# A three-block kernel in float32r parts: low parts of the normalised values on VectorE instead of GpSimd, and the output weights' conversion behind the input projection

## The chip, the cores and the metric

The kernel runs on one core of a Trainium2 chip. The metric is device time in microseconds (us). The engines are TensorE (PE; PEld are its weight loads), VectorE (DVE), ScalarE (ACT), GpSimd (POOL) and SyncE (SP), which issues most of the DMAs. Each engine works through its own instructions in the order in which they stand, and waits for the others by semaphores.

## The reference

Two sequences of 768 tokens with 8 heads of 48 go through three blocks: a linear attention with a state that decays, a Fourier mixing with an MLP, and a spatially gated MLP. The change lies in the third:

```python
def _moe2_ref(x, w_in, g_ln, w_sg, b_sg, w_out):
    h = x @ w_in                                   # [2, 768, 384] @ [384, 1024]
    h = gelu_tanh(h)
    u, v = (h[..., :d_ff // 2], h[..., d_ff // 2:])
    mu = np.mean(v, axis=-1, keepdims=True)
    var = np.mean((v - mu) ** 2, axis=-1, keepdims=True)
    v_n = (v - mu) / np.sqrt(var + 1e-06) * g_ln
    v_s = np.einsum('ts,bsd->btd', w_sg, v_n) + b_sg[None, :, None]
    gated = u * v_s
    return (x + gated @ w_out).astype(np.float32)
```

## The kernel before

TensorE multiplies float32r. To keep float32's precision, every operand of a large product is split in two parts: the high part is the value rounded to float32r, the low part is what is left. A product then takes three matmuls, hi x hi, hi x lo and lo x hi (`mm3`, line 110, where all of them are counted). Names that end in `_hi` and `_lo` are these parts.

The third block is written in `gating`, for batch 0 and then for batch 1:

- `gate_in` makes v for each of six chunks of 128 tokens, t = 0 to 5. TensorE writes `v_ps` (nine matmuls of 512 columns), ScalarE takes the gelu (L575), VectorE the statistics (L577, L579), GpSimd the reciprocal deviation `rs` in two short operations (L581, L582), VectorE normalises in place (L583), ScalarE casts the high part `vn_hi` (L585), and L586 subtracts it to get the low part `vn_lo`.
- `u_in` makes u: eight tiles `u_ps`, nine matmuls of 384 columns each, and a gelu on ScalarE (L596).
- `spatial` multiplies by `w_sg` over the tokens: for each of four feature blocks f and two halves of the tokens, 18 matmuls into `s_ps`, which need vn of all six chunks; then g, b and u on VectorE (L609, L610), and the split of the gated product (L612 on ScalarE, L613 on GpSimd), which takes vn's place.
- `project` multiplies by `w_out` into `o_ps`; VectorE adds x (L624), and a DMA writes the result.

The weights arrive as float64 bits. `load_split` turns 384 columns of them into float32 by three integer operations on VectorE (L157, L158, L159, out `st`), a cast on ScalarE (L163) and a subtraction on GpSimd (L164); `wout` takes four such steps, `late_weights`. `wsg` arrives as float32 and takes a cast and the subtraction only. `raw` and `st` have two buffers each.

Buffers that matter here: the tiles v, t_g and o share the tag "tb" with three buffers, so v of chunk t + 3 may be written when the low part of chunk t has been made. `v_ps`, `u_ps` and `o_ps` share five PSUM banks (tag "g"), `s_ps` has three (tag "c").

The order of instructions isn't that of the code alone. `merge(a, b, 1.0)` writes one step of b behind each step of a, and a list scheduler (Tile, with its own timeline as a guess) then puts the instructions of each engine in order, the earlier written one first where several are ready.

Of the kernel before, what the change touches and what calls it, by code (L numbers as in the profile page):

```python
# [70 lines left out]
# keeps the logarithm finite where a product vanishes  # L71
TINY = 1e-37
# brings any variance into the range of the logarithm
FAR = 2.0 ** -64
# how far a pair's sum over its tokens of P * (1 / P) may lie from their number
# [6 lines left out]
class Split:  # L82
    """An operand as the exact sum of two float32r parts."""
# [13 lines left out]
def fused(ctx, tc, ins, out, dbg=None):  # L97
    nc = tc.nc
# [19 lines left out]
    # ---- constants that stay  # L118
# [27 lines left out]
    def load_split(w, src, o, at, raw=None):  # L146
        """Load NST columns and split them; float64 arrives as raw bits and becomes float32 first."""
# [23 lines left out]
    # ---- attention  # L171
    def prep(n, b, p, ap):
        if b == 0:
            # every pair of the first batch has room of its own: that of later tiles
# [10 lines left out]
        # the first pair in two parts: the start is shorter  # L185
# [10 lines left out]
        for c0, c1 in parts:  # L196
# [6 lines left out]
            # decays from the start of each chunk: P[t] up to before t, P[t + 1] up to and with t  # L203
# [8 lines left out]
            # r and k change sign, both  # L212
# [13 lines left out]
    def own_term(ap, n, b, p, prod, v):  # L226
        """The current token's own term: dv = (sum_d r u k) v."""
# [10 lines left out]
        for c in range(NC_):  # L238
            # the columns after the first two are overwritten: a stream of fewer than 96 takes as long
            nc.tensor.matmul(dg_ps[:, 2 * c:2 * c + 2 * D], lhsT=prod[:, c], rhs=uh[:, None, 2 * p:2 * p + 2].to_broadcast([PR, D, 2]), start=True, stop=True)  # L240
# [8 lines left out]
    def scores(ap, c0, rt, kt):  # L249
        """Scores of chunks c0..c0+2, of the earlier tokens alone."""  # L250
        res = []
        sc_pss = [gps.tile([C, 3, C], F32, name="sc_ps", tag="g") for h in range(2)]
        for i, h in [(i, h) for i in range(3) for h in range(2)] if IL else [(i, h) for h in range(2) for i in range(3)]:
            c = c0 + i
            # the two heads lie in different halves of the array's rows
# [9 lines left out]
    def chunk_states(ap, b, ends, kt, v, U):  # L265
        """States before chunks 1..5: U[j] = P_end[j] * (U[j - 1] + sum_s k v)."""
# [19 lines left out]
    def values(b, c0, rt, sc, v, dv, U, yo):  # L286
        y_ps = ps(b, [C, 512], "y_ps", YB)
        # between the two heads' columns a block that no one reads: both heads' values go through, in the time of one's
# [9 lines left out]
    def radix6(x, y, Z, es, G):  # L298
        """Over the token chunks: x = (a, b), a = y_c + y_c+3, b = +-(y_c - y_c+3);
        Z = sum (Z0, Z3), real (Z2, Z1), imaginary (Z2, Z1; the factors are in the DFT's constants)."""  # L300
# [10 lines left out]
    def attention(ap, yz):  # L311
        """Both batches' pairs of heads, in one pipeline; yields the batch that is through."""
        pairs = [(b, p) for b in range(B) for p in range(NP)]

        def junk(m, l, r):
            """Matmuls that no one reads, where the tensor engine would wait: its clock halves if it idles."""
# [696 lines left out]
```

## Time and profile before

| | |
|---|---|
| median of 3 timed runs | 476.03 us (474.46 to 479.01) |
| span of the profiled execution | 483.4 us; no time of its own is listed beside it |
| TensorE busy | 443.2 us (92%) |
| VectorE busy | 310.9 us (64%) |
| GpSimd busy | 213.1 us (44%) |
| ScalarE busy | 170.0 us (35%) |
| mean granted TensorE clock | 0.881 of full speed |

The profiled execution is another one than the timed ones, and its span is 7.4 us longer than their median. Matmuls are pipelined: a matmul's duration in the timeline is longer than the distance from its start to that of the next, and the distance is what the stream costs. The granted clock is 1.00 (2.4 GHz) or 0.50 (1.2 GHz); a value between is a mean over a stretch. In the timeline the bracket at the end of a row is the time for which the engine stood idle before it, and who released it.

### The profile page before, as it was taken

Reading aid. Unit: us, or ns where it says so; the run is one execution under the profiler, and the core shown is the slowest. Engines: PE = TensorE matmul, PEld = TensorE weight load, DVE = VectorE, ACT = ScalarE, POOL = GpSimd, SP = SyncE. Lnnn points to the kernel's source line nnn. Section 1 sums busy time; section 2 is a strip of 40 time slices with the busy share of each in tenths; the row PEclk is TensorE's granted clock in tenths of the full one; section 3 lists DMA queues with packets and bytes.
Section 4 is the critical chain, followed back from the end, with each engine's and each line's share of the span. In section 5 each row is a group of like instructions: output and inputs, shape, how many; then the busy total and the mean of one; then the engine's idle time right before and its main releaser. Section 6 shows DMA issues by size and latency. Waiting matters only on the chain.

```text
span 483.4 us, 6594 instructions
## 1 busy us (share of the span) xinstructions
PE 443.2 (92%) x2474; PEld 418.3 (87%) x2474; DVE 310.9 (64%) x518; ACT 170.0 (35%) x389; POOL 213.1 (44%) x206
## 2 busy tenths in 40 slices
PE   9689989978869997698999999999999799999995
PEld 8578978977769987598999899999889698999995
DVE  5999799599797899959874531631369334611332
ACT  3542433553543423543424311522364212311110
POOL 1658876468593474634231200201478525700330
PEclk9765555595979999899999999999999799999998
DMA  7932694032225332310050000001333000020002
GB/s 204 273 93 84 204 295 139 1 110 77 68 82 169 127 98 62 77 58 1 6 143 18 0 1 0 1 1 34 95 104 97 0 1 0 18 83 0 2 12 94
DMA packets 13641, 35.41 MB, mean 73 GB/s; under 512 B 1760, under 2 KB 5632, under 8 KB 13472
## 3 DMA queue, kind: packets, MB, share of 16 engines
q1 hardware_dynamic: 13456, 32.54, 22.9%
q0 software_dynamic: 144, 2.36, 1.4%
q8 instruction: 21, 0.34, 0.3%
q14 instruction: 20, 0.16, 0.1%
HBM read 32.53 MB, written 2.36 MB: 72 GB/s over the span
## 4 chain that ended last, share of the span: by engine, by line
PE 48%; DVE 24%; issue 10%; DMA 7%; POOL 6%; ACT 3%; SPq 1%; POOLq 0%; DVEq 0%; ACTq 0%
PE s_ps L110 10%; PE z_ps L110 6%; PE o_ps L110 5%; PE ch L110 5%; PE y_ps L295 4%; PE sc_ps L257 3%; DVE st L158 3%; PE u_ps L110 3%; PE v_ps L110 3%; PE x_ps L110 3%; DMA raw<-in_wsg 2%; DVE st L159 2%; DVE st L157 2%; PE y_ps L293 2%; DMA rk<-in_rk 2%
## 5 line engine op out<-in xcount | busy, mean ns | idle before, releaser
L110 PE MATMUL z_ps<-us_hi,w 128*128 128x384 f32 x288 | 80.7, 344 | 4.2 <-ACT us_hi L499 4.0
L110 PE MATMUL ch<-z_hi,w 128*128 128x384 f32 x288 | 80.5, 339 | 3.1 <-ACT z_hi L523 3.0
L524 DVE SCALAR_TENSOR_TENSOR z_lo<-z_ps,z_hi 128x384 fp32r<-128x384 f32 x48 | 26.6, 554 | 56.1 <-ACT z_hi L523 56.1
L110 PEld LDWEIGHTS z_ps<-us_hi,w 128*128 128x128 f32 x288 | 53.9, 193 | 5.4 <-ACT us_hi L499 4.6
L110 PEld LDWEIGHTS ch<-z_hi,w 128*128 128x128 f32 x288 | 52.4, 189 | 4.8 <-ACT z_hi L523 4.6
L110 PE MATMUL ch<-z_lo,w 128*128 128x384 f32 x144 | 49.2, 342 | 4.1 <-DVE z_lo L524 4.0
L110 PE MATMUL z_ps<-us_lo,w 128*128 128x384 f32 x144 | 48.9, 340 | 0.0
L164 POOL TENSOR_TENSOR w<-st,w 128x384 fp32r<-128x384 f32 x24 | 31.4, 1310 | 31.8 <-ACT w L163 31.8
L523 ACT ACTIVATE z_hi<-z_ps 128x384 fp32r<-128x384 f32 x48 | 23.6, 492 | 59.2 <-PE z_ps L110 45.3
L613 POOL TENSOR_TENSOR vn_lo<-t_g,vn_hi 128x384 fp32r<-128x384 f32 x16 | 16.1, 1016 | 55.6 <-ACT vn_hi L612 55.6
L609 DVE SCALAR_TENSOR_TENSOR t_g<-s_ps,g,bsg 128x384 f32<-128x384 f32 x16 | 9.6, 617 | 47.3 <-PE s_ps L110 47.3
L110 PE MATMUL s_ps<-wsg_hi,vn_hi 128*128 128x384 f32 x96 | 33.7, 351 | 2.7 <-ACT vn_hi L585 2.7
L261 POOL TENSOR_SCALAR_AFFINE_SELECT sc<-sc 128x384 f32<-128x384 f32 x32 | 28.5, 911 | 16.8 <-ACT sc L260 16.6
L110 PE MATMUL s_ps<-wsg_hi,vn_lo 128*128 128x384 f32 x96 | 33.8, 352 | 1.1 <-POOL vn_lo L586 1.1
L110 PE MATMUL s_ps<-wsg_lo,vn_hi 128*128 128x384 f32 x96 | 33.6, 350 | 0.0
L110 PEld LDWEIGHTS ch<-z_lo,w 128*128 128x128 f32 x144 | 27.0, 188 | 6.4 <-DVE z_lo L524 6.3
L295 PE MATMUL y_ps<-v,sc 128*128 128x96 f32 x144 | 28.9, 334 | 0.0
L110 PEld LDWEIGHTS z_ps<-us_lo,w 128*128 128x128 f32 x144 | 27.8, 193 | 0.0
L295 PEld LDWEIGHTS y_ps<-v,sc 128*128 128x128 f32 x144 | 27.2, 254 | 0.6 <-issue 0.4
L164 POOL TENSOR_TENSOR wsg_lo<-raw,wsg_hi 128x384 fp32r<-128x384 f32 x12 | 12.4, 1036 | 32.5 <-ACT wsg_hi L163 32.3
L476 POOL TENSOR_TENSOR z_lo<-uc,z_hi 128x384 fp32r<-128x384 f32 x7 | 7.4, 1056 | 38.4 <-ACT z_hi L475 38.4
L257 PE MATMUL sc_ps<-rk 48*128 48x128 f32 x144 | 20.7, 358 | 3.5 <-DVE rk L218 3.5
(232 smaller groups left out, 1131.4 us busy)
## 6 DMA issues: line engine op xcount, KB each, us to landing
raw<-in_w SPq DMA_DIRECT2D x12, 384.0 KB, 3.9
w_raw<-in_w SPq DMA_DIRECT2D x12, 384.0 KB, 5.2
rk<-in_rk SPq DMA_DIRECT2D x5, 672.0 KB, 5.4
raw<-in_win SPq DMA_DIRECT2D x8, 384.0 KB, 3.3
prod<-in_ruk SPq DMA_DIRECT2D x4, 624.0 KB, 3.9
dft<-in_dft POOLq DMA_DIRECT2D x1, 2304.0 KB, 11.1
raw<-in_wsg SPq DMA_DIRECT2D x12, 192.0 KB, 2.4
out<-o SPq DMA_DIRECT2D x12, 192.0 KB, 1.9
```

Of the source, the lines that this page charges most:

```text
L110: nc.tensor.matmul(o, lhsT=x, rhs=y, start=start and i == 0, stop=stop and i == len(ps) - 1)
L157: nc.vector.tensor_scalar(out=st, in0=top, scalar1=3, scalar2=0x3FFFFFF8, op0=ALU.logical_shift_left, op1=ALU.bitwise_and)
L158: nc.vector.scalar_tensor_tensor(out=st, in0=top, scalar=0xC0000000, in1=st, op0=ALU.bitwise_and, op1=ALU.bitwise_or)
L159: nc.vector.scalar_tensor_tensor(out=st, in0=low, scalar=29, in1=st, op0=ALU.logical_shift_right, op1=ALU.bitwise_or)
L164: nc.gpsimd.tensor_tensor(out=w.lo[:, to], in0=x, in1=w.hi[:, to].bitcast(F32), op=ALU.subtract)
L257: nc.tensor.matmul(sc_pss[h][:, i, :], lhsT=kt[hs, c * C:(c + 1) * C], rhs=rt[hs, c, :], start=True, stop=True)
L261: nc.gpsimd.affine_select(out=sc, in_=sc, pattern=[[0, 3], [1, C]], compare_op=ALU.is_gt, fill=0.0, base=0, channel_multiplier=-1)
L293: nc.tensor.matmul(y3[:, i, 0:3:2], lhsT=rt[:, c, :], rhs=U[:, :, c - 1], start=True, stop=True)
L295: nc.tensor.matmul(y3[:, i, h:h + 2], lhsT=sc[h][:, i, :], rhs=v[:, c], start=c == 0, stop=True, skip_group_check=c > 0)
L523: nc.scalar.activation(out=z.hi, in_=z_ps, func=AF.Relu)
L524: nc.vector.scalar_tensor_tensor(out=z.lo, in0=z_ps, scalar=0.0, in1=z.hi.bitcast(F32), op0=ALU.max, op1=ALU.subtract)
L613: nc.gpsimd.tensor_tensor(out=vn.lo[:, f, 3 * h:3 * h + 3], in0=th, in1=vn.hi[:, f, 3 * h:3 * h + 3].bitcast(F32), op=ALU.subtract)
```

## The change

The low part of the normalised values (L586) goes from GpSimd to VectorE, in both batches. The steps of `late_weights` are written behind the steps of batch 0's `spatial`, not of its `gate_in`. The rest of the diff takes comments out.

```diff
@@ def gate_in(mp2, x2, win, vn):
             vf = v.rearrange("p (f e) -> p f e", f=NF2)
             nc.scalar.copy(vn.hi[:, :, t], vf)
-            nc.gpsimd.tensor_tensor(out=vn.lo[:, :, t], in0=vf, in1=vn.hi[:, :, t].bitcast(F32), op=ALU.subtract)
+            nc.vector.tensor_tensor(out=vn.lo[:, :, t], in0=vf, in1=vn.hi[:, :, t].bitcast(F32), op=ALU.subtract)
             yield
@@ def gating(mp2, win, x2, wsg, then=None):
         u2 = u2t()
-        merge(gate_in(mp2, x2[0], win, vn[0]), late_weights(), 1.0)
+        run(gate_in(mp2, x2[0], win, vn[0]))
         run(u_in(mp2, x2[0], win, u2))
-        run(spatial(mp2, vn[0], u2, wsg, g, bsg))
+        merge(spatial(mp2, vn[0], u2, wsg, g, bsg), late_weights(), 1.0)
```

The order of SyncE's DMAs is the same in both kernels. On TensorE the order differs between batch 0's u_ps and s_ps. Before, the scheduler puts pieces of s_ps between the u_ps tiles (3325 is the third u_ps tile, 3391 the first half of s_ps for f = 0; vn_hi and vn_lo are one tile for all chunks):

```order
L110 MATMUL u_ps_3314<-x2_0_lo_2265,win_hi_2262 128x384
L110 MATMUL u_ps_3314<-x2_0_hi_2264,win_lo_2263 128x384
L110 MATMUL s_ps_3391<-wsg_hi_2983,vn_hi_3134 128x384 [waits DMAHW4_49,DMAHW3_49,DMAHW5_49,DMAHW2_49,DMAHW6_49,DMAHW1_49,DMAHW7_49,DMAHW0_49,Activation_49]
L110 MATMUL s_ps_3391<-wsg_lo_2984,vn_hi_3134 128x384 [waits Pool_49]
L110 MATMUL s_ps_3391<-wsg_hi_2983,vn_lo_3135 128x384 [waits Pool_49]
L110 MATMUL u_ps_3325<-x2_0_hi_2264,win_hi_2262 128x384 [waits Activation_49]
L110 MATMUL u_ps_3325<-x2_0_lo_2265,win_hi_2262 128x384
```

In the changed kernel the tiles are numbered anew (3282 is the second u_ps tile, 3293 the third), and the third follows the second at once:

```order
L110 MATMUL u_ps_3282<-x2_0_lo_2265,win_hi_2262 128x384
L110 MATMUL u_ps_3282<-x2_0_hi_2264,win_lo_2263 128x384
L110 MATMUL u_ps_3293<-x2_0_hi_2264,win_hi_2262 128x384 [waits Activation_49]
L110 MATMUL u_ps_3293<-x2_0_lo_2265,win_hi_2262 128x384
L110 MATMUL u_ps_3293<-x2_0_hi_2264,win_lo_2263 128x384
```

All eight u_ps tiles now stand ahead of the first s_ps, and s_ps waits for VectorE (DVE) where it waited for GpSimd (Pool). The wait of the third u_ps tile is for the bank of v(3), that of the fourth for v(4), that of the fifth for v(5).

On VectorE, batch 0's chunks 2 to 5 stand like this before (v2_3209, 3239, 3269 and 3291 are v of chunks 2 to 5; st_3162 and 3192 are the first two steps of wout):

```order
L583 TENSOR_SCALAR v2_3209<-v2_3209,mv_3213,rs_3215 128x512 [waits DVE_49,Pool_49]
L577 BN_STATS stt_3241<-v2_3239 128x6 [waits Activation_49]
L157 TENSOR_SCALAR st_3162<-raw_3161 128x384 [waits DMAHW6_49]
L579 BN_AGGR mv_3243<-stt_3241 128x2 [waits DVE_49]
L158 SCALAR_TENSOR_TENSOR st_3162<-raw_3161,st_3162 128x384 [waits DVE_49]
L159 SCALAR_TENSOR_TENSOR st_3162<-raw_3161,st_3162 128x384 [waits DVE_49]
L577 BN_STATS stt_3271<-v2_3269 128x6 [waits Activation_49]
L157 TENSOR_SCALAR st_3192<-raw_3191 128x384 [waits DMAHW7_49]
```

And in the changed kernel (v2_3149, 3171, 3193, 3215, 3237 are v of chunks 0 to 4; st_3408 is the first step of wout):

```order
L586 TENSOR_TENSOR vn_lo_3135<-v2_3149,vn_hi_3134 128x4x128 [waits Activation_49]
L583 TENSOR_SCALAR v2_3193<-v2_3193,mv_3197,rs_3199 128x512 [waits DVE_49,Pool_49]
L586 TENSOR_TENSOR vn_lo_3135<-v2_3171,vn_hi_3134 128x4x128 [waits Activation_49]
L577 BN_STATS stt_3217<-v2_3215 128x6 [waits Activation_49]
L586 TENSOR_TENSOR vn_lo_3135<-v2_3193,vn_hi_3134 128x4x128 [waits Activation_49]
L157 TENSOR_SCALAR st_3408<-raw_3407 128x384 [waits DMAHW6_49]
L579 BN_AGGR mv_3219<-stt_3217 128x2 [waits DVE_49]
L577 BN_STATS stt_3239<-v2_3237 128x6 [waits Activation_49]
L158 SCALAR_TENSOR_TENSOR st_3408<-raw_3407,st_3408 128x384 [waits DVE_49]
```

The low parts stand among the statistics; the first steps of wout still stand among the work on chunks 3 to 5.

On GpSimd, the end of batch 0's `gate_in` before (rs_3275 and 3297 belong to chunks 4 and 5):

```order
L582 TENSOR_TENSOR rs_3275<-rs_3275,mhalf_71 128x1 [waits Pool_49]
L164 TENSOR_TENSOR wout_lo_3129<-st_3192,wout_hi_3128 128x384 [waits Activation_49]
L586 TENSOR_TENSOR vn_lo_3135<-v2_3239,vn_hi_3134 128x4x128 [waits Activation_49]
L581 TENSOR_SCALAR rs_3297<-mv_3295 128x1 [waits DVE_49]
L586 TENSOR_TENSOR vn_lo_3135<-v2_3269,vn_hi_3134 128x4x128 [waits Activation_49]
L164 TENSOR_TENSOR wout_lo_3129<-st_3222,wout_hi_3128 128x384 [waits Activation_49]
L582 TENSOR_TENSOR rs_3297<-rs_3297,mhalf_71 128x1 [waits Pool_49]
```

And in the changed kernel (rs_3243 and 3265 belong to chunks 4 and 5):

```order
L581 TENSOR_SCALAR rs_3243<-mv_3241 128x1 [waits DVE_49]
L582 TENSOR_TENSOR rs_3243<-rs_3243,mhalf_71 128x1 [waits Pool_49]
L581 TENSOR_SCALAR rs_3265<-mv_3263 128x1 [waits DVE_49]
L582 TENSOR_TENSOR rs_3265<-rs_3265,mhalf_71 128x1 [waits Pool_49]
L164 TENSOR_TENSOR wout_lo_3129<-st_3408,wout_hi_3128 128x384 [waits Activation_49]
```

No low part of vn stands there any more, and the four wout parts follow the last rs.

## Rows read from the trace of the kernel before

**Rows 1.** The page: the span, and the chain that ended last, by engine.

```profile
span 483.4 us, 6594 instructions
...
PE 48%; DVE 24%; issue 10%; DMA 7%; POOL 6%; ACT 3%; SPq 1%; POOLq 0%; DVEq 0%; ACTq 0%
```

**Rows 2.** Stretches: each engine's busy us (instructions), granted clock, DMA share, GB/s.

```profile
358.00:361.00 3.00, 2.06 (x11) 1.48 (x10) 0.70 (x3) 1.28 (x3) 2.46 (x4) 1.00 0.45 134
...
380.00:382.00 2.00, 2.00 (x6) 2.00 (x7) 0.88 (x2) 0.00 (x0) 0.00 (x0) 0.50 0.00 0
...
385.00:386.00 1.00, 1.00 (x7) 1.00 (x6) 0.00 (x0) 0.00 (x0) 0.47 (x1) 0.96 0.00 0
...
410.00:425.00 15.00, 15.00 (x81) 14.18 (x80) 9.18 (x17) 4.79 (x8) 10.73 (x14) 1.00 0.11 40
```

**Rows 3.** Timeline of TensorE, 355 to 385: start, duration, engine, line, idle before.

```profile
355.67 0.33 PE L110 MATMUL u_ps<-x_hi,win_hi 128*128 128x384 f32 x1
...
360.09 0.44 PE L110 MATMUL s_ps<-wsg_hi,vn_lo 128*128 128x384 f32 x1 [0.76 <-POOL vn_lo L586]
...
366.61 0.34 PE L110 MATMUL u_ps<-x_lo,win_hi 128*128 128x384 f32 x1
...
370.95 0.34 PE L110 MATMUL u_ps<-x_hi,win_lo 128*128 128x384 f32 x1
...
375.54 0.34 PE L110 MATMUL s_ps<-wsg_hi,vn_lo 128*128 128x384 f32 x1
378.62 0.69 PE L110 MATMUL s_ps<-wsg_hi,vn_hi 128*128 128x384 f32 x1 [2.74 <-ACT vn_hi L585]
...
379.97 0.69 PE L110 MATMUL s_ps<-wsg_hi,vn_lo 128*128 128x384 f32 x1 [0.35 <-POOL vn_lo L586]
380.46 0.52 PE L110 MATMUL s_ps<-wsg_hi,vn_hi 128*128 128x384 f32 x1
...
384.62 0.52 PE L110 MATMUL s_ps<-wsg_lo,vn_hi 128*128 128x384 f32 x1
```

**Rows 4.** Timeline of GpSimd, 358 to 377.

```profile
358.76 1.27 POOL L586 TENSOR_TENSOR vn_lo<-v,vn_hi 128x512 fp32r<-128x512 f32 x1
359.99 0.57 POOL L582 TENSOR_TENSOR rs<-rs,mhalf 128x1 f32<-128x1 f32 x1
360.53 1.01 POOL L164 TENSOR_TENSOR wsg_lo<-raw,wsg_hi 128x384 fp32r<-128x384 f32 x1
...
374.82 1.32 POOL L164 TENSOR_TENSOR wout_lo<-st,wout_hi 128x384 fp32r<-128x384 f32 x1
376.11 0.56 POOL L582 TENSOR_TENSOR rs<-rs,mhalf 128x1 f32<-128x1 f32 x1
```

**Rows 5.** Timeline of VectorE, 353 to 362.

```profile
353.54 0.54 DVE L564 TENSOR_TENSOR x_lo<-uT,x_hi 128x384 fp32r<-128x384 f32 x1
...
354.16 1.22 DVE L564 TENSOR_TENSOR x_lo<-uT,x_hi 128x384 fp32r<-128x384 f32 x1
...
358.13 0.17 DVE L579 BATCH_NORM_AGGREGATE mv<-stt 128x2 f32<-128x6 f32 x1
360.60 1.22 DVE L583 TENSOR_SCALAR v<-v,mv,rs 128x512 f32<-128x512 f32 x1 [2.29 <-POOL rs L582]
```

**Rows 6.** Timeline of ScalarE: the gelu of chunk 3.

```profile
360.06 0.60 ACT L575 ACTIVATE v<-v_ps 128x512 f32<-128x512 f32 x1 [1.20 <-POOL vn_lo L586]
```

**Rows 7.** Groups by line and shape, whole run: busy us, mean ns, idle before.

```profile
L429 DVE TENSOR_TENSOR Xl<-x_ps,Xh 128x512 fp32r<-128x512 f32 x3 | 2.0, 678 | 0.0
```

**Rows 8.** The same groups, 335 to 425 us alone.

```profile
L583 DVE TENSOR_SCALAR v<-v,mv,rs 128x512 f32<-128x512 f32 x12 | 11.0, 917 | 7.0 <-POOL rs L582 6.8
...
L577 DVE BATCH_NORM_STATS2 stt<-v 128x6 f32<-128x512 f32 x12 | 8.2, 687 | 6.9 <-ACT v L575 6.9
...
L158 DVE SCALAR_TENSOR_TENSOR st<-raw,st 128x384 uint32<-128x384 uint32 x4 | 5.0, 1247 | 0.0
...
L159 DVE SCALAR_TENSOR_TENSOR st<-raw,st 128x384 uint32<-128x384 uint32 x4 | 3.2, 797 | 0.1
```

## The prediction, made before the change was run

> **What bounds the kernel now.** I read the page first: its span and the chain that ended last put about half of the 483.4 us on TensorE [rows 1]. Order and timeline differ from the changed kernel only from the gated block on, so I then read stretches of it by window. TensorE is full in most of them; in batch 1's input projection it is busy for 15.00 of 15.00 us at full clock [rows 2]. There a faster VectorE or GpSimd can give nothing. The one place of the block, before its tail, where TensorE stands still is between batch 0's input products and its spatial products, 355.7 to 385 us [rows 3].
>
> There I size what can be won. From 355.67 to 378.62 TensorE issues 102 matmuls: 72 of u_ps and 30 of s_ps. Undisturbed, u_ps go out every 0.1736 us (25 steps from 366.61 to 370.95) and s_ps every 0.1765 us (26 steps from 370.95 to 375.54) [rows 3]. 72 x 0.1736 + 30 x 0.1765 = 17.8 us, so the 103rd could start at 373.47; it starts at 378.62. That is **5.15 us of waiting**, of which 2.74 us is one wait for the normalised values of the last token chunk, t = 5. Another 0.35 us follows at 379.97, for that chunk's low part. While TensorE stood still its granted clock fell to 0.50, and it is back near 1 only at 385 [rows 2]: in that stretch s_ps go out every 0.32 us (13 steps from 380.46 to 384.62), 0.1435 more than normal, for about 19 matmuls, which is **2.7 us**. Together 5.15 + 0.35 + 2.7 = 8.2 us can be won here, and after this place TensorE stays full, so what is won reaches the end.
>
> Why t = 5 is late is read on the other engines. The v tiles have three buffers, so v(t + 3) starts on ScalarE when the low part of chunk t is done. GpSimd makes that part of t = 0 from 358.76 to 360.03, and v(3) starts at 360.06 [rows 4, 6]. For t = 5 the reciprocal deviation (L582) stands behind a wout low part on GpSimd and runs at 376.11 [rows 4]; normalising, the cast and the low part can only follow it.
>
> **The change, part by part.** *Low parts to VectorE.* GpSimd loses twelve operations (six in each batch) of 1.27 us as the row at 358.76 has it; VectorE gains twelve. VectorE has no such row before. Nearest is its subtraction of the same size with one operand from PSUM, 0.68 us [rows 7]; but here both come from SBUF, and that kind takes 0.54 us for 384 columns when it starts before a GpSimd operation, and 1.22 us when it starts behind one (x_lo at 353.54 and at 354.16 [rows 5]), 0.68 more. So a low part costs 0.68 to about 1.7 us (0.68 plus a whole wsg part of 1.0 us on GpSimd, the row at 360.53 [rows 4]). I take 0.68, since on GpSimd only the short rs pairs and two wsg parts are left in this stretch.
>
> The Trainium skill speaks against this edit: its page "SBUF — State Buffer", section "Who interferes with whom", says that a VectorE instruction with two SBUF inputs contends with a GpSimd instruction that reads SBUF, and that the later one fully blocks. The trace agrees, by the 0.54 and 1.22 us. By that rule a low part behind a wsg part would pay the upper price, and by the quiet row the lower; the sum below goes by the rows.
>
> Step by step, in batch 0. Chunk 0: VectorE is free at about 358.25 (after the aggregation at 358.13, 0.17 us), its low part ends at 358.93 instead of 360.03, v(3) takes 0.60 us and ends at 359.58. The third u_ps group needs the PSUM bank that v(3) leaves. TensorE gets there at 355.67 + 18 x 0.1736 = 358.79 and goes on at 359.65: a wait of 0.85 us. Chunk 1: its low part stands behind L583 of chunk 2 on VectorE, which waits for rs(2). GpSimd now makes rs(2) without a 1.27 us low part ahead, so at about 359.75 instead of 360.56 [rows 4]; L583 takes 1.22 us beside the wsg part, as in [rows 5], so the low part runs from 361.0 to 361.7, and v(4) ends at 362.35. TensorE reaches the fourth group at 359.65 + 9 x 0.1736 = 361.21: it waits 1.2 us. Chunk 2: after a statistics operation of 0.69 us its low part ends at 363.0 and v(5) at 363.65; TensorE needs that bank at 363.98 and doesn't wait. The fifth group on needs only u values that ScalarE has by then. So **2.05 us of waiting** remain, and u_ps end at 370.2.
>
> Then the spatial products. Now all 72 u_ps come ahead of the first s_ps; two s_ps pieces that filled time between u_ps before no longer do. Chunk t is wanted at 370.2 + 6 t x 0.1765, chunk 5 at 375.5. After 363.0 VectorE has, up to the low part of chunk 5: three L157, two L158 and two L159 for wout, two statistics, three aggregations, three L583 and three low parts. At the means of this stretch, which the contention inflates (0.80 for L157 too, 1.25, 0.80, 0.69, 0.17, 0.92, and 0.68 for the low parts [rows 5, 7, 8]), that is 2.4 + 2.5 + 1.6 + 1.4 + 0.5 + 2.8 + 2.0 = 13.2 us, to 376.2, which would cost 0.7 us. At their quiet durations (0.54 us for two-input operations of 384 columns [rows 5], no longer for L157 and L583) it is 3 x 0.54 + 4 x 0.54 + 1.4 + 0.5 + 1.6 + 2.0 = 9.3, to 372.3. I take the latter, since GpSimd makes no low part there now, and allow 0.2 for the waits between: 372.5, three microseconds early.
>
> *Output weights.* The diff moves the conversion behind the input projection. But the order of SyncE is the same word for word, so their DMAs start where they did, and on VectorE the first wout operations still stand among those of chunks 3 to 5. Only GpSimd's four wout parts stand behind all of rs now. That is what frees rs(5) from its place behind a 1.32 us wout part (at 374.82 [rows 4]); by itself it costs nothing, since o_ps, which reads wout, starts after batch 1's v_ps. If that cover went, 4 x 1.0 us of GpSimd would show.
>
> *Batch 1.* VectorE gets six low parts, 6 x 0.68 = 4.1 us, in a stretch where it works 9.18 of 15 us and TensorE is full [rows 2]: no gain, and no cost.
>
> Sum: 8.2 - 2.05 = 6.15 us less, if the clock doesn't fall in the two waits. A wait of 0.76 us with a smaller one behind it left the granted clock at 1.00 in 358 to 361 [rows 2, 3], so I take that it doesn't. The profiled execution's span is 7.4 us longer than the median of the timed runs, 476.03, and no time of its own is given; I subtract the same microseconds from the median, since the waits hang on durations of operations, and get **469.9 us**. About 1% (4.8 us) is what a measurement can tell from no change.
>
> **The rivals.** *The clock wasn't down in the timed runs, or falls again in the new waits.* Then only the idle time counts: 6.15 - 2.7 = 3.45, 472.6 us. For it: the profiled execution is slower than all timed ones (474.46 to 479.01). Against: the 2.74 us wait is made of dependences that every run has. Chance 0.15.
>
> *The low parts pay the upper price where they gate.* Each of the three pays a whole GpSimd operation, 1.0 us: v(5) ends at 366.65, TensorE starts that group 2.7 us later, the gain is 3.45 again, or 0.75 if the clock falls too: 472.6 to 475.3. For it stands x_lo's 1.22; against, that only two wsg parts are left to collide with. Chance 0.14. The skill's rule just named is this rival if every collision is lost.
>
> *VectorE becomes the bound, and it is slower.* VectorE is strictly in order here: what waits holds up all behind it. If each of the six low parts of batch 0 loses against a GpSimd operation as long as the wout part at 374.82 [rows 4], it pays 0.68 + 1.32 = 2.0 us. The three gates come 3 x 1.32 = 4.0 us late, of which TensorE had 0.3 to spare at v(5): 3.7 more waiting, and the clock falls, 2.7 more. With the wout operations at their inflated means, chunk 5 is done at 363.0 + 4.0 + 13.2 + 4.0 = 384.2; TensorE wants it at 375.5 + 3.7 + 2.7 = 381.9, waits 2.3 us, and the clock falls again: 2.05 + 3.7 + 2.7 + 2.3 + 2.7 = 13.45 us lost against 8.2 before, 481.3 us. It decides from about 1.9 us for each low part on; below that the loss stays under 1%. Against it: GpSimd's own work there shrinks to two wsg parts, the short rs operations and the four wout parts. Chance 0.07.
>
> *The second edit does nothing and the first only moves a wait* (u_ps wait for VectorE instead of GpSimd, no s_ps to fill in, chunk 5 still late by VectorE's queue): 475 to 476. Against it: chunk 5's slack of three microseconds. Chance 0.06.
>
> **How the numbers follow.** The forecast (467.5 to 471.2, by both ends of the low parts' quiet price and of the clock's share) has 0.58. The range goes from 466.8, nearly all 8.2 us and a microsecond of the median's own spread, to 475.3, the second rival's end. Faster by over 1% is the forecast and a little of the first two rivals, 0.61; within 1% are the rest of these and the fourth, 0.32; slower is the third, 0.07.
>
> **What would show it.** Right: L586 on VectorE at about 0.7 us; no TensorE wait over 1.5 us between u_ps and s_ps; the granted clock at 1.00 through that stretch; u_ps all ahead of s_ps, with two waits, for v(3) and v(4). Wrong: L586 above 1.2 us; s_ps waiting for chunk 5; the granted clock at 0.50 after the input products; or a wait in batch 1 where there was none.

## The result, and the profile after

The kernel changed runs in 0.987 of the time before, 95% interval 0.984 to 0.991: 475.46 us median of 20 runs against 479.1 of 20 beside them. The ratio is of the undisturbed runs of each kernel alone, while over all 20 runs the medians lie 3.6 us apart and the means 5.0. At a ratio of 0.9872 the change takes 6.1 us off 479.1; the forecast was 6.15. The page's span and the engines' shares of the chain that ended last, for [rows 1]:

```profile
span 472.5 us, 6597 instructions
...
PE 41%; DVE 33%; issue 10%; DMA 7%; POOL 4%; ACT 3%; SPq 1%; POOLq 0%; DVEq 0%; ACTq 0%
```

The span is 10.9 us shorter than before, but that isn't the change alone: batch 0's first u_ps starts at 351.54 here and at 355.67 before [rows 3], and up to there the order is the same. The granted clock up to that point was 0.87 here and 0.85 before. So I measure from that matmul on. To the start of the last o_ps matmul it is 466.51 - 351.54 = 114.97 us after, and 477.42 - 355.67 = 121.75 us before, **6.78 us less**. Two more rows of before, batch 1's first v_ps and the last o_ps:

```profile
386.37 0.48 PE L110 MATMUL v_ps<-win_hi,x_hi 128*128 128x512 f32 x1
...
477.42 0.34 PE L110 MATMUL o_ps<-vn_hi,wout_lo 128*128 128x384 f32 x1
```

TensorE's timeline after, for [rows 3]:

```profile
351.54 0.33 PE L110 MATMUL u_ps<-x_hi,win_hi 128*128 128x384 f32 x1
...
354.52 0.34 PE L110 MATMUL u_ps<-x_hi,win_lo 128*128 128x384 f32 x1
355.27 0.44 PE L110 MATMUL u_ps<-x_hi,win_hi 128*128 128x384 f32 x1 [0.42 <-ACT v L575]
...
356.80 0.34 PE L110 MATMUL u_ps<-x_hi,win_lo 128*128 128x384 f32 x1
357.87 0.44 PE L110 MATMUL u_ps<-x_hi,win_hi 128*128 128x384 f32 x1 [0.73 <-ACT v L575]
...
365.60 0.34 PE L110 MATMUL u_ps<-x_hi,win_lo 128*128 128x384 f32 x1
365.78 0.34 PE L110 MATMUL s_ps<-wsg_hi,vn_hi 128*128 128x384 f32 x1
...
375.42 0.48 PE L110 MATMUL v_ps<-win_hi,x_hi 128*128 128x512 f32 x1
...
466.51 0.34 PE L110 MATMUL o_ps<-vn_hi,wout_lo 128*128 128x384 f32 x1
```

Two waits are left, for v(3) and v(4). The starts come 354.52 to 355.27 and 356.80 to 357.87, less a step of 0.1736 each: 0.58 + 0.90 = 1.47 us. No s_ps waits. The whole gain lies ahead of batch 1's first v_ps: that starts 30.70 us behind the first u_ps before and 23.88 us after, and from there to the last o_ps it takes 91.05 and 91.09 us. The stretches, for [rows 2]:

```profile
353.00:356.00 3.00, 2.58 (x15) 2.26 (x14) 2.23 (x4) 1.93 (x4) 2.38 (x4) 1.00 0.44 117
356.00:359.00 3.00, 2.27 (x13) 1.94 (x12) 3.00 (x7) 1.81 (x4) 0.46 (x2) 1.00 0.56 149
...
380.00:395.00 15.00, 15.00 (x82) 14.39 (x81) 5.50 (x10) 3.01 (x6) 4.26 (x5) 1.00 0.00 0
...
399.00:414.00 15.00, 15.00 (x81) 14.18 (x80) 10.60 (x22) 4.57 (x8) 3.46 (x8) 1.00 0.13 46
```

The clock stays at 1.00 where it was 0.50, through the two waits too. In the last row, in which five of batch 1's six low parts are made, TensorE is full. VectorE's timeline, for [rows 5]:

```profile
353.88 0.65 DVE L586 TENSOR_TENSOR vn_lo<-v,vn_hi 128x512 fp32r<-128x512 f32 x1
355.30 1.23 DVE L583 TENSOR_SCALAR v<-v,mv,rs 128x512 f32<-128x512 f32 x1 [0.77 <-POOL rs L582]
356.44 0.68 DVE L586 TENSOR_TENSOR vn_lo<-v,vn_hi 128x512 fp32r<-128x512 f32 x1
...
363.85 1.37 DVE L159 SCALAR_TENSOR_TENSOR st<-raw,st 128x384 uint32<-128x384 uint32 x1
...
367.30 0.68 DVE L586 TENSOR_TENSOR vn_lo<-v,vn_hi 128x512 fp32r<-128x512 f32 x1
```

The last row is chunk 5's low part, done at 367.98. GpSimd in the same stretch, for [rows 4]:

```profile
355.23 1.01 POOL L164 TENSOR_TENSOR wsg_lo<-raw,wsg_hi 128x384 fp32r<-128x384 f32 x1
...
360.75 1.36 POOL L581 TENSOR_SCALAR rs<-mv 128x1 f32<-128x1 f32 x1 [1.11 <-DVE mv L579]
...
363.14 0.62 POOL L582 TENSOR_TENSOR rs<-rs,mhalf 128x1 f32<-128x1 f32 x1
363.73 1.08 POOL L164 TENSOR_TENSOR wout_lo<-st,wout_hi 128x384 fp32r<-128x384 f32 x1
```

rs(5) runs at 363.14, 11.6 us behind the first u_ps; before it was 376.11 [rows 4], 20.4 us behind it. And ScalarE, whose gelu of v(3) follows chunk 0's cast and low part, for [rows 6]:

```profile
354.62 0.60 ACT L575 ACTIVATE v<-v_ps 128x512 f32<-128x512 f32 x1
```

VectorE's groups from 335 to 425 us, for [rows 7, 8]:

```profile
L586 DVE TENSOR_TENSOR vn_lo<-v,vn_hi 128x512 fp32r<-128x512 f32 x12 | 8.1, 676 | 0.9 <-ACT vn_hi L585 0.8
L583 DVE TENSOR_SCALAR v<-v,mv,rs 128x512 f32<-128x512 f32 x12 | 7.8, 647 | 2.1 <-POOL rs L582 2.0
...
L158 DVE SCALAR_TENSOR_TENSOR st<-raw,st 128x384 uint32<-128x384 uint32 x4 | 2.2, 548 | 0.0
```

The twelve low parts cost 676 ns each, as estimated from 678. Their neighbours got cheaper: L583 from 917 to 647 ns, L158 from 1247 to 548.

### The profile page after: what moved, and what is told of

Its sections match the earlier page's. It is cut to its first block, busy times and chain, and to the rows that moved or that the text cites. A ratio compares the mean times of both kernels' runs of the same rounds, so it can differ in the third digit from the quotient of the medians.

```text
span 472.5 us, 6597 instructions
## 1 busy us (share of the span) xinstructions
PE 431.3 (91%) x2474; PEld 409.4 (87%) x2474; DVE 314.5 (67%) x530; ACT 169.3 (36%) x389; POOL 195.2 (41%) x194
## 4 chain that ended last, share of the span: by engine, by line
PE 41%; DVE 33%; issue 10%; DMA 7%; POOL 4%; ACT 3%; SPq 1%; POOLq 0%; DVEq 0%; ACTq 0%
PE s_ps L110 11%; PE o_ps L110 5%; PE z_ps L110 5%; PE ch L110 5%; PE u_ps L110 4%; DVE st L158 3%; DVE st L159 3%; PE v_ps L110 3%; DVE st L157 2%; PE y_ps L295 2%; DMA raw<-in_wsg 2%; DVE rk L218 2%; DVE U L281 2%; DMA rk<-in_rk 2%; DVE P L204 2%
## 5 line engine op out<-in xcount | busy, mean ns | idle before, releaser
L613 POOL TENSOR_TENSOR vn_lo<-t_g,vn_hi 128x384 fp32r<-128x384 f32 x16 | 16.1, 1017 | 58.0 <-ACT vn_hi L612 58.0
L261 POOL TENSOR_SCALAR_AFFINE_SELECT sc<-sc 128x384 f32<-128x384 f32 x32 | 26.2, 839 | 17.5 <-ACT sc L260 17.4
L110 PE MATMUL s_ps<-wsg_hi,vn_lo 128*128 128x384 f32 x96 | 32.4, 338 | 0.0
L110 PE MATMUL s_ps<-wsg_lo,vn_hi 128*128 128x384 f32 x96 | 32.4, 338 | 0.0
L110 PE MATMUL s_ps<-wsg_hi,vn_hi 128*128 128x384 f32 x96 | 32.4, 338 | 0.0
L257 PEld LDWEIGHTS sc_ps<-rk 48*128 48x128 f32 x144 | 16.7, 250 | 12.7 <-DVE rk L218 9.7
L295 PE MATMUL y_ps<-v,sc 128*128 128x96 f32 x144 | 26.9, 316 | 0.0
L295 PEld LDWEIGHTS y_ps<-v,sc 128*128 128x128 f32 x144 | 25.5, 237 | 0.5 <-issue 0.2
```

The costliest lines, as they stand in the source:

```text
L110: nc.tensor.matmul(o, lhsT=x, rhs=y, start=start and i == 0, stop=stop and i == len(ps) - 1)
L257: nc.tensor.matmul(sc_pss[h][:, i, :], lhsT=kt[hs, c * C:(c + 1) * C], rhs=rt[hs, c, :], start=True, stop=True)
L261: nc.gpsimd.affine_select(out=sc, in_=sc, pattern=[[0, 3], [1, C]], compare_op=ALU.is_gt, fill=0.0, base=0, channel_multiplier=-1)
L295: nc.tensor.matmul(y3[:, i, h:h + 2], lhsT=sc[h][:, i, :], rhs=v[:, c], start=c == 0, stop=True, skip_group_check=c > 0)
L613: nc.gpsimd.tensor_tensor(out=vn.lo[:, f, 3 * h:3 * h + 3], in0=th, in1=vn.hi[:, f, 3 * h:3 * h + 3].bitcast(F32), op=ALU.subtract)
```

## The experiments

The theory: batch 0's low parts, on GpSimd, were the way by which chunk 5 came late (they free v's buffers, and stand ahead of rs), and moving them is the whole gain. Rivals: the second edit has a part in it; only v's buffers, or only GpSimd's full queue, is the cause; TensorE's new order (all u_ps ahead of the first s_ps) is; the clock isn't lost by the wait.

For all kernels, from batch 0's first u_ps to the last o_ps and to the end of the span, in the profiled execution; then TensorE's waits between u_ps and s_ps by the list of waits, the granted clock's lowest level behind them, and the timed runs. The list counts a wait from the modelled end of the matmul before it, so it has 1.1 us where the starts above gave 1.47. The kernel before beside a run was timed anew in each set.

| kernel | to last o_ps | to the end | waits | clock | median, before beside it | ratio (95%) |
|---|---|---|---|---|---|---|
| before | 121.75 | 127.73 | s 2.7 + 1.1, u 0.2 | 0.50 | | |
| changed | 114.97 | 120.96 | u 1.1 | 1.00 | 475.46, 479.1 | 0.987 (0.984 to 0.991) |
| e1_low_alone | 115.02 | 121.17 | u 1.2 | 1.00 | 472.68, 479.61 | 0.980 (0.974 to 0.986) |
| e2_wout_alone | 120.82 | 126.88 | s 2.7 + 1.3, u 0.2 | 0.50 | 480.97, 479.61 | 0.987 (0.979 to 0.995) |
| e2_again | 122.12 | 128.19 | s 2.7 + 1.3, u 0.2 | 0.50 | 478.1, 480.45 | 0.998 (0.993 to 1.004) |
| e3_filler | 119.41 | 125.52 | s 1.4, u 0.2 | 1.00 | 477.32, 479.61 | 0.996 (0.992 to 1.000) |
| e6_pool_busy | 115.82 | 122.02 | s 0.9, u 0.9 | 1.00 | 473.48, 479.61 | 0.982 (0.975 to 0.990) |
| e10_gates_alone | 115.92 | 123.06 | u 1.2, s 0.7 | 1.00 | 473.59, 483.49 | 0.985 (0.977 to 0.992) |
| e9_rooms_gpsimd | 119.85 | 126.21 | s 2.4 + 0.2, u 1.1 | 0.50 | 479.23, 483.49 | 0.992 (0.986 to 0.997) |
| e11_three_rooms_gpsimd | 117.42 | 123.75 | s 1.8, u 0.2 | 0.61 | 476.48, 482.12 | 0.990 (0.984 to 0.995) |
| e4_five_rooms | 113.98 | 120.58 | u 0.4 | 1.00 | 471.74, 480.45 | 0.987 (0.981 to 0.993) |
| e12_three_rooms | 113.24 | 119.73 | none | 1.00 | 474.73, 482.12 | 0.990 (0.981 to 0.999) |
| e8_gated_vector | 113.96 | 120.38 | u 0.4 | 1.00 | 472.16, 480.45 | 0.984 (0.979 to 0.990) |
| e5_batch0_alone | 115.15 | 122.20 | u 1.3 | 1.00 | 474.89, 480.45 | 0.988 (0.980 to 0.996) |

0.61 is the mean of a stretch of 2.5 us that holds part of the fall. The ratios of small sets scatter by more than the differences looked for, so the verdicts go by the stretch to the last o_ps. From there to the end it is 5.98 to 7.14 us, most of it behind the last operation of any engine. From batch 1's first v_ps to the last o_ps every one of these kernels takes 91.05 to 91.10 us, so all their differences arise between batch 0's first u_ps and that v_ps. The order of before ran three times (before and the second edit alone) and takes 120.82 to 122.12 us, the changed order twice, 114.97 and 115.02: the gain of 6.78 is one pair of executions out of 5.8 to 7.2.

**The first edit alone.**

```diff
-            nc.gpsimd.tensor_tensor(out=vn.lo[:, :, t], in0=vf, in1=vn.hi[:, :, t].bitcast(F32), op=ALU.subtract)
+            nc.vector.tensor_tensor(out=vn.lo[:, :, t], in0=vf, in1=vn.hi[:, :, t].bitcast(F32), op=ALU.subtract)
```

> The first edit alone: low parts of the normalised values on VectorE, output weights converted where the kernel before has them. Its order of instructions is that of the changed kernel on every engine. Theory (the first edit is all of the change): the ratio to the kernel before is that of the full change, 0.987 within the measurement's 0.4%; from the first u_ps product of batch 0 to the end of the span it takes 121 us against 127.7 before, with two or three TensorE waits for ScalarE's v (L575) of 1.5 to 2.1 us together, no s_ps wait, and the granted clock at 1.00 from there on. Rival (the prediction's word that the second edit frees rs(5)): a wait for chunk 5 of 1 us or more comes back, the time to the end is 123 us or more and the ratio 0.992 or more.

115.02 us and the same two waits: the first edit is the whole gain. In the trace every compute engine has the instructions of the changed kernel in the same order. The ratio is 0.7% below the whole change's all the same; I put that down to the scatter of six runs.

**The second edit alone, twice.**

```diff
-        merge(gate_in(mp2, x2[0], win, vn[0]), late_weights(), 1.0)
+        run(gate_in(mp2, x2[0], win, vn[0]))
...
-        run(spatial(mp2, vn[0], u2, wsg, g, bsg))
+        merge(spatial(mp2, vn[0], u2, wsg, g, bsg), late_weights(), 1.0)
```

> The second edit alone: output weights converted behind batch 0's input projection, low parts of the normalised values on GpSimd as before. Its order of instructions is that of the kernel before. Theory (the second edit does nothing): ratio 1.000 within 0.5%, 127.7 us from the first u_ps product of batch 0 to the end within 0.7, the s_ps wait for the normalised values of chunk 5 at 2.7 us and the granted clock at 0.50 right behind it. Rival (it frees rs(5)): that wait falls below 1.5 us, and the stretch takes 126 us or less.

> The second edit alone once more, since its first timing had a median above that of the kernel before (480.97 against 479.61 us) and yet a ratio of 0.987, an interval of 1.6% from three runs on its side. Theory (the second edit moves no instruction, so it does nothing): 127 us from the first u_ps product of batch 0 to the end (within 0.9 of 126.9 and 127.7), the wait for chunk 5 at 2.7 us, ratio 1.00 within 0.6%. Rival (it gains by itself, where the first timing is believed): ratio 0.987 again, with no shorter wait that could account for it.

Chunk 5 is waited for as before, in the first and in the second execution:

```profile
372.86 0.44 PE L110 MATMUL s_ps<-wsg_hi,vn_hi 128*128 128x384 f32 x1 [2.74 <-ACT vn_hi L585]
...
370.25 0.45 PE L110 MATMUL s_ps<-wsg_hi,vn_hi 128*128 128x384 f32 x1 [2.73 <-ACT vn_hi L585]
```

The second timing gives 0.998, and the first one's 0.987, whose median lies above that of before, was scatter. The edit does nothing: in both traces every compute engine has the instructions of the kernel before in the same order, so the list scheduler puts them back where they were.

Between these two executions of one kernel lies 1.30 us, nearly all of it in how long the clock stayed down behind the same wait. Stretches of the first, behind its wait that ended at 372.86:

```profile
375.12:377.62 2.50, 2.50 (x10) 2.50 (x9) 2.05 (x4) 0.48 (x1) 0.00 (x0) 0.50 0.00 0
377.62:380.12 2.50, 2.50 (x16) 2.50 (x15) 0.14 (x1) 0.53 (x2) 2.00 (x2) 1.00 0.00 0
```

And of the second, behind its wait that ended at 370.25:

```profile
372.41:374.91 2.50, 2.50 (x9) 2.50 (x9) 2.15 (x4) 0.37 (x1) 0.00 (x0) 0.50 0.00 0
374.91:377.41 2.50, 2.50 (x9) 2.50 (x9) 0.01 (x1) 0.63 (x2) 1.98 (x2) 0.50 0.00 0
```

In the timeline 9 s_ps steps are of 0.32 us in the one and 17 in the other; at 0.1435 us lost each, that is 1.3 and 2.4 us. In the kernel before there were 14.

**The wait filled with products that nobody reads.** It adds 16 matmuls and leaves the result as it is.

```diff
+                if f == 0 and s == NC_ - 2 and fill:
+                    jp = gps.tile([C, 512], F32, name="jp2", tag="g")
+                    for i in range(fill):
+                        nc.tensor.matmul(jp[:, :HT], lhsT=vn.hi[:, f, s], rhs=wsg.hi[:, s * S:s * S + HT], start=True, stop=True)
...
-        run(spatial(mp2, vn[0], u2, wsg, g, bsg))
+        run(spatial(mp2, vn[0], u2, wsg, g, bsg, 16))
```

> The kernel before with 16 products added in batch 0, behind the products of chunk 4 for the first channel tile: each 384 columns wide, into a PSUM bank that nobody reads, in the place where TensorE waits 2.74 us for chunk 5. 16 x 0.177 us = 2.8 us of work that the result doesn't need. Theory (the clock is lost because TensorE stands still there): the wait is filled, the granted clock stays at 1.00 up to 385, and the stretch from the first u_ps product to the end takes 2.7 us less than before, about 125.0 us, although TensorE does more. Rival 1 (the clock falls for another reason): the clock is at 0.50 there all the same and the stretch takes 127.7 us. Rival 2 (the clock falls whenever TensorE waits, also in the shorter waits ahead): it is below 1.00 from an earlier place on.

The stretch behind the filler and a last wait of 0.73 us, in this kernel:

```profile
374.28:376.78 2.50, 2.50 (x17) 2.50 (x16) 1.85 (x4) 1.00 (x2) 0.44 (x1) 1.00 0.02 7
```

The clock stays up, and the stretch to the last o_ps is 2.34 us shorter than before's, 1.41 and 2.71 shorter than the second edit's two executions, with more work done. Both rivals fall: it is the idle time that costs the clock, and the shorter waits (up to 0.73 us here) don't. The filler takes the place of the 2.74 us wait (16 x 0.177 = 2.8), so all that is won is the clock.

**GpSimd as full as before.** Each chunk of batch 0 gets a subtraction of 128x512 more on GpSimd, whose result isn't used.

```diff
+            if dup is not None:
+                nc.gpsimd.tensor_tensor(out=dup.lo[:, :, t], in0=vn.hi[:, :, t].bitcast(F32), in1=vn.hi[:, :, t].bitcast(F32), op=ALU.subtract)
...
-        run(gate_in(mp2, x2[0], win, vn[0]))
+        run(gate_in(mp2, x2[0], win, vn[0], vn[1]))
```

> The changed kernel with one GpSimd subtraction of 128x512 added for each of batch 0's six chunks, where the low part stood before; its result isn't used (it is overwritten before anything reads it). VectorE makes the low parts as in the changed kernel, and GpSimd is as full as before. Theory (the gain comes from the low part being out of GpSimd's queue, so that rs of the next chunks comes early, and from v's buffers coming free early): v(3) still starts early, but rs of chunks 2 to 5 stand behind a 1.27 us subtraction each and VectorE collides with it, so that low parts take up to 1.7 us; 2 to 5 us of the gain of 6.6 are lost: 123 to 126 us from the first u_ps product to the end, and TensorE waits for chunk 5 again. Rival (only the low part's own place counts, and GpSimd's fullness is without effect): 121 us as in the changed kernel, ratio 0.987.

A miss: I expected 2 to 5 us lost, and it is 0.85. TensorE does wait for chunk 5 again, and a low part collides, as the theory had it. VectorE's row, started behind a GpSimd subtraction at 366.49:

```profile
366.74 1.52 DVE L586 TENSOR_TENSOR vn_lo<-v,vn_hi 128x512 fp32r<-128x512 f32 x1
```

TensorE's row, its whole price:

```profile
370.50 0.44 PE L110 MATMUL s_ps<-wsg_hi,vn_lo 128*128 128x384 f32 x1 [0.86 <-DVE vn_lo L586]
```

rs(5) runs 14.6 us behind the first u_ps here, against 11.6 in the changed kernel and 20.4 before. With the low parts on VectorE, a full GpSimd by itself matters little.

**Only the three low parts that free a buffer.**

```diff
-            nc.gpsimd.tensor_tensor(out=vn.lo[:, :, t], in0=vf, in1=vn.hi[:, :, t].bitcast(F32), op=ALU.subtract)
+            (nc.vector if t < early else nc.gpsimd).tensor_tensor(out=vn.lo[:, :, t], in0=vf, in1=vn.hi[:, :, t].bitcast(F32), op=ALU.subtract)
...
-        merge(gate_in(mp2, x2[0], win, vn[0]), late_weights(), 1.0)
+        merge(gate_in(mp2, x2[0], win, vn[0], 3), late_weights(), 1.0)
```

> The kernel before with only the low parts of batch 0's chunks 0, 1 and 2 on VectorE, those that free the buffers of v(3), v(4) and v(5); chunks 3 to 5 and all of batch 1 stay on GpSimd. Theory (these three carry the whole gain): two u_ps waits of 1.5 us together as in the changed kernel, no s_ps wait, and 114.9 to 115.8 us from the first u_ps product to the last o_ps product, against 114.97 in the changed kernel. Rival (chunk 5's own queue on GpSimd, with wout parts and low parts ahead of it, is a cause of its own): s_ps waits of 1 us or more for chunks 4 or 5 remain, 117 us or more.

115.92 us: 5.83 of the 6.78. An s_ps wait of 0.7 us for a low part from GpSimd remains, so the three carry 86% of the gain and not quite all.

**Buffers alone, low parts on GpSimd.** First two, then three more places for v of batch 0:

```diff
-            v = mp2.tile([C, DH2], F32, name="v2", tag="tb", bufs=3)
+            v = room[:, 3 - t, :DH2] if room is not None and t < 2 else mp2.tile([C, DH2], F32, name="v2", tag="tb", bufs=3)
...
-        merge(gate_in(mp2, x2[0], win, vn[0]), late_weights(), 1.0)
+        merge(gate_in(mp2, x2[0], win, vn[0], u2), late_weights(), 1.0)
```

> The kernel before, low parts on GpSimd and output weights where they were, with two more places for v in batch 0 (chunks 0 and 1 in the part of u2 that u fills later). Theory (what binds is that v's three buffers are freed by the low parts, not that GpSimd is full): v(3) and v(4) start without waiting, statistics and rs of chunks 3 to 5 come earlier, and the 2.74 us wait for chunk 5 goes without any edit to the low parts; one u_ps wait of up to 1.6 us for v(5) remains. From the first u_ps product of batch 0 to the last o_ps product 115 to 116.5 us, against 121.75 before and 114.97 in the changed kernel. Rival (GpSimd is what is full: its low parts hold up rs however many buffers there are): chunk 5 is late still, with an s_ps wait of 1.5 us or more and the clock falling behind it, 118 us or more.

The rival's result: 119.85 us, chunk 5 late by 2.4 us still. But v(5) was not free there, it waited for chunk 2's low part until 366.8. So the third place, with `room` the flat second half of u2 and `t < 3`:

```diff
+            v = room[:, t * DH2:(t + 1) * DH2] if room is not None and t < 3 else mp2.tile([C, DH2], F32, name="v2", tag="tb", bufs=3)
...
+        merge(gate_in(mp2, x2[0], win, vn[0], u2[:, 2:].rearrange("p f s -> p (f s)")), late_weights(), 1.0)
```

> The kernel before with three more places for v in batch 0 (chunks 0 to 2 in the part of u2 that u fills later), so that none of the six v waits for a low part; low parts on GpSimd, output weights where they were. Two more places left a wait of 2.4 us for chunk 5, with v(5) still behind the low part of chunk 2. Theory (v's buffers, freed by a GpSimd queue, are what the first edit loosens): with the third place too the s_ps wait for chunk 5 falls under 0.5 us, and from the first u_ps product of batch 0 to the last o_ps product it takes 114 to 115.5 us. Rival (GpSimd's queue itself, in which rs stand behind low parts and wout parts, makes chunk 5 late): v(5) starts early, but chunk 5 is waited for by 1 us or more, 117 us or more.

117.42 us, 4.33 less than before. The rival named the time and the length of the wait rightly, but not the chunk: the wait of 1.77 us is for chunk 4's low part, and chunk 5 isn't waited for. ScalarE's cast of chunk 4 in this kernel:

```profile
363.39 0.62 ACT L585 CAST vn_hi<-v 128x512 fp32r<-128x512 f32 x1 [0.92 <-DVE v L583]
```

GpSimd's timeline:

```profile
363.03 1.21 POOL L164 TENSOR_TENSOR wout_lo<-st,wout_hi 128x384 fp32r<-128x384 f32 x1
364.20 0.57 POOL L582 TENSOR_TENSOR rs<-rs,mhalf 128x1 f32<-128x1 f32 x1
364.73 1.36 POOL L164 TENSOR_TENSOR wout_lo<-st,wout_hi 128x384 fp32r<-128x384 f32 x1
366.05 3.00 POOL L586 TENSOR_TENSOR vn_lo<-v,vn_hi 128x512 fp32r<-128x512 f32 x2
```

And TensorE's:

```profile
367.55 0.44 PE L110 MATMUL s_ps<-wsg_hi,vn_lo 128*128 128x384 f32 x1 [1.77 <-POOL vn_lo L586]
```

With v free, rs(5) (364.20) still stands behind a wout part, and the last two low parts behind another: chunk 4's could start when its cast ends at 364.01, and starts at 366.05. Neither "only buffers" nor "only the queue" holds: buffers alone give 4.33 of 6.78, and by these rows the queue is what keeps the rest. TensorE has the order of the changed kernel here, so the order isn't the gain either: with it and the low parts on GpSimd, 2.45 us are still missing.

**Buffers on top of the change.** The same two edits to v's places, two and three, in the changed kernel.

> The changed kernel with two more places for v in batch 0: chunks 0 and 1 have theirs in the part of u2 that u fills only later, so v(3) and v(4) no longer wait for the low parts of chunks 0 and 1. Theory (what is left of the waits is v's three buffers): both TensorE waits for L575 go, 0.6 + 0.9 us of lost starts, and from the first u_ps product to the end it takes 119.5 us against 121.0 in the changed kernel, ratio to the kernel before 0.984. Rival (VectorE's queue is what is late, and only shows elsewhere): the same 1.5 us come back as a wait of s_ps for chunks 3 to 5, and the stretch takes 121 us.

> The changed kernel with the same three places for v, to see whether anything is left of v's buffers beside the two places already tried (113.98 us to the last o_ps product). Theory (v(5) did not wait for its buffer in the changed kernel): no more than 0.3 us less than with two places, 113.7 to 114.1 us. Rival (the wait of 0.4 us for a u value that was left goes with it): 113.5 us or less.

Two places take both v waits away, but win 1.0 us, not 1.5: a wait of 0.4 us for a u value takes their place. With three places nothing waits. Its first 15 us of u_ps and s_ps:

```profile
349.57:364.57 15.00, 15.00 (x88) 15.00 (x87) 14.51 (x29) 8.28 (x17) 9.99 (x15) 1.00 0.43 120
```

And the first u_ps and batch 1's first v_ps:

```profile
349.57 0.33 PE L110 MATMUL u_ps<-x_hi,win_hi 128*128 128x384 f32 x1
...
371.72 0.48 PE L110 MATMUL v_ps<-win_hi,x_hi 128*128 128x512 f32 x1
```

113.24 us to the last o_ps, 1.73 less than in the changed kernel, the best of all here; its rival was right. By the timed runs (0.990, up to 0.999) it can't be told from the changed kernel.

**Gated low parts on VectorE too**, on top of the two places.

```diff
-                nc.gpsimd.tensor_tensor(out=vn.lo[:, f, 3 * h:3 * h + 3], in0=th, in1=vn.hi[:, f, 3 * h:3 * h + 3].bitcast(F32), op=ALU.subtract)
+                nc.vector.tensor_tensor(out=vn.lo[:, f, 3 * h:3 * h + 3], in0=th, in1=vn.hi[:, f, 3 * h:3 * h + 3].bitcast(F32), op=ALU.subtract)
```

> The kernel with two more places for v and, besides, the low parts of the gated values (L613, 128x384) on VectorE, not GpSimd. Theory: GpSimd took 1.02 us for one, VectorE takes 0.55 for such a size, and the last of them stands in the chain that ended last, before the last products: 0.5 us less than the kernel with two more places, 119.0 us from the first u_ps product to the end, ratio 0.983. Rival (VectorE, fuller by 24 operations of 0.55 us, becomes late in batch 1, where it has 11.7 of 15 us): a TensorE wait for VectorE appears and the stretch takes 120 us or more.

L613 went from 1017 to 556 ns, and the stretch from 113.98 to 113.96 us. A miss: that operation isn't on the path that sets the end. VectorE, fuller, makes nobody wait either.

**Batch 1's low parts back on GpSimd.**

```diff
-            nc.vector.tensor_tensor(out=vn.lo[:, :, t], in0=vf, in1=vn.hi[:, :, t].bitcast(F32), op=ALU.subtract)
+            lo.tensor_tensor(out=vn.lo[:, :, t], in0=vf, in1=vn.hi[:, :, t].bitcast(F32), op=ALU.subtract)
...
-        run(gate_in(mp2, x2[0], win, vn[0]))
+        run(gate_in(mp2, x2[0], win, vn[0], nc.vector))
...
-        run(gate_in(mp2, x2[1], win, vn[1]))
+        run(gate_in(mp2, x2[1], win, vn[1], nc.gpsimd))
```

> The changed kernel with batch 1's six low parts back on GpSimd. Theory (batch 1's input projection has TensorE full, so its part of the first edit is worth nothing): 121.0 us from the first u_ps product of batch 0 to the end, within 0.7, and a busy share of TensorE of 15.00 in 15.00 us there; ratio as the whole change, 0.987. Rival (batch 1 has its part of the gain, or pays): the stretch is 1 us or more away from 121.0, with a wait in batch 1's u_ps or s_ps.

To the end, which the expectation names, it is 122.20 us, and the rival's 1 us is there; but to the last o_ps it is 115.15 against 114.97 and 115.02, with no wait in batch 1. The difference lies behind the last VectorE operation, which ends at 470.28, 6.1 us before the span does (5.05 in the changed kernel), where this edit has no instruction. From batch 1's first v_ps to the last o_ps it is 91.10 us, against 91.09 in the changed kernel, so batch 1's part is worth nothing; the 0.2 us lie ahead of it.

## Why the prediction was right, step by step

**What can be won, 8.2 us: right, a little small, and not the same in every execution.** The kernel without any wait (e12_three_rooms) starts batch 1's first v_ps 371.72 - 349.57 = 22.15 us behind the first u_ps; before it was 30.70. That is 8.55 us, and 7.59 and 8.88 us in the two executions of the second edit alone, which have the same order. What is short is the clock's 2.7 us: the 24 s_ps from 378.62 to 386.23 took 3.37 us more than at 0.1765 each, and less the wait of 0.35 that is 3.0. The rival that the clock wasn't down in the timed runs falls, for this order: those two executions are timed ones (478.8 and 477.44 us), and the clock is at 0.50 in both.

**The low part's price, 0.68 us: right**, 0.65 to 0.68 in batch 0. The prediction's rival of upper prices didn't come about, but not because the collisions are gone: L583 beside a wsg part took 1.23 us, L159 beside a wout part 1.37, so other operations pay. It is a matter of what starts first: in e6_pool_busy a low part behind a GpSimd subtraction took 1.52, inside my bounds of 0.68 to 1.7. The rule of the Trainium skill's page "SBUF — State Buffer", section "Who interferes with whom", that of two which contend the later one blocks for all of the other's time, agrees with the 1.23 (its GpSimd operation ran from 355.23 to 356.24, and L583 ended 0.29 us behind that) and the 1.52.

**The two waits, 0.85 + 1.2 us: the place right, the size too large.** They measured 0.58 + 0.90. Counted from the first u_ps, v(3) ended at 3.68 us (forecast 3.91), v(4) at 6.27 (6.68) and v(5), with no wait as forecast, at 7.47 (7.98). The u_ps ended at 14.24 (14.5), and all that the changed kernel loses to the one without waits is 23.88 - 22.15 = 1.73 us, against 2.05. So two terms of the sum were off, each by about 0.3 us and both to the same side: what is lost before (8.55 against 8.2) and what stays (1.73 against 2.05). The clock held at 1.00 in both waits, as I had taken.

**Chunk 5's three microseconds: right.** Its low part was done 16.44 us behind the first u_ps (forecast 16.8), and was wanted at 14.24 + 30 x 0.1765 = 19.5. The quiet durations were the right choice for L157 and L158 (0.56 and 0.55 us); L159 (0.76) and batch 0's L583 (0.75) still collided in places.

**The output weights: the price right, the reason wrong.** "That is what frees rs(5) from its place behind a 1.32 us wout part" is the sentence that failed. I read the whole difference of GpSimd's order as the second edit's. Alone, that edit leaves the order of before, and the first edit alone gives the order of the changed kernel: with v's low parts gone from GpSimd, rs go ahead of the wout parts by themselves. That they do so because chunks 3 to 5 come earlier in the scheduler's own timeline is my reading; that timeline isn't shown here. The fourth rival, to which I gave 0.06, was right in its first half: the second edit does nothing.

**Batch 1: no gain and no cost, right**, to 0.05 us (91.05 and 91.09 us from its first v_ps to the last o_ps). The row that I read for its input projection, 410 to 425 us [rows 2], holds only the end of that, to 414.57, and then batch 0's o_ps; TensorE is full in both.

**The number of microseconds.** By the ratio it is 6.1 for a forecast of 6.15, by the stretch 6.78. That the first comes within 0.05 us is luck: the ratio's interval is 4.4 to 7.9 us, and the medians of all runs give 3.6. The times themselves moved: before had a median of 476.03 us in three runs and of 479.1 in twenty, and 475.46 lies just above the 475.3 at which the range ended.

So the mechanism is: chunk t's low part on GpSimd freed the buffer of v(t + 3), and stood with others ahead of rs. VectorE makes it in 0.68 us, not 1.27, and GpSimd is left with rs. The three gates' move alone gives 5.83 us. Four kernels set the two ways side by side: three more places for v alone give 4.33 us (121.75 to 117.42), the change alone 6.78, both 8.51 (to 113.24). So where no v waits for its buffer, the change still gives 4.18 us, by GpSimd's queue and the low part's price, the clock that they cost included; where the low parts are on VectorE, the places still give 1.73; and some 2.6 us either of them wins. No kernel here emptied the queue and left v's buffers as tight as before.

## What to carry to other kernels

An engine with a low busy share can set the time if what it makes frees a buffer: ask who may only start when this operation ends, and move that one first (three of twelve operations gave 86% here). Where a scheduler sets the order, build each half of a change alone and compare the orders before you credit it: one of two edits here moved nothing. And where the clock in the earlier part of the kernel differs from run to run, measure from a fixed instruction behind it.

## What the runs showed that I had not expected

- Up to batch 0's first u_ps the kernel before and the second edit alone have one order, yet that matmul came at 355.67 (clock 0.85 up to there) and at 347.41 us (0.91): 8.3 us, more than the whole change.
- A wait of 1.77 us was enough for the clock to fall to half (e11_three_rooms_gpsimd, 0.61 in 367.5 to 370), while none of the waits up to 0.9 us between u_ps and s_ps did it.
- The GpSimd operation at 360.75, 128x1, took 1.36 us; the one before it and the one behind it (358.77 and 362.83) took 0.22. It ended at 362.11, and VectorE ran three operations back to back from 360.59 to 362.04, of which none is longer than 0.55. In e1_low_alone, which has the same order, it took 1.35 us again (362.58). That one VectorE operation after the other kept it out is my reading; nothing here isolates it.
- VectorE took on 8.1 us of low parts, and from the first u_ps on it is busy only 0.7 us longer (52.4 against 51.7): L583 (11.0 to 7.8 us) and L158 (5.0 to 2.2) gave back 6.0. In e6_pool_busy, with a subtraction for each chunk on GpSimd again, batch 0's L583 took 1112 ns each against 753 in the changed kernel, so a part of what they had cost was GpSimd's subtractions beside them. The totals of the whole run, 314.5 and 310.9, hold 2.9 us more ahead of the first u_ps, where the order is the same in both.
